# Result stores of one batch's 64 rows each, in place of stores over two batches' 128 rows

## The chip, the cores and the metric

The kernel runs on one core of a Trainium2 chip. A core has a matrix engine (PE, whose weight loads are shown as PEld), three engines for elementwise work (DVE, ACT, POOL), a queue engine (SP) that here does nothing but start DMAs, and 16 DMA engines that carry them out. The metric is the device time of one execution in microseconds (us); the median over runs is given, lower is better.

## The reference, cut to what matters

Two blocks follow each other: a linear attention with a decaying state (4 batches, 8 heads, 768 steps, 48 features a head) and a feed-forward block on its 3072 output rows of 384 features.

```python
B, H, S, D = 4, 8, 768, 48                       # then 3072 rows, d_model 384, d_ff 1536
for t in range(S):
    cur = einsum('bhd,bhe->bhde', u[None] * k[:, :, t], v[:, :, t])
    y[:, :, t] = einsum('bhd,bhde->bhe', r[:, :, t], state + cur)
    state = w[None, :, :, None] * state + einsum('bhd,bhe->bhde', k[:, :, t], v[:, :, t])
x = y.transpose(0, 2, 1, 3).reshape(B * S, H * D)  # row b*768 + t
xn = x / sqrt(mean(x * x) + 1e-6) * rms_g
g = xn @ w_gate
out = (g * sigmoid(g) * (xn @ w_val)) @ w_out
```

The weights of the second block arrive as float64, the rest as float32.

## The kernel before

**Tiling.** Time is cut into 12 chunks `s` of 64 steps (`L`); one chunk holds 64 rows of each of the 4 batches, 256 rows of the result. `mixing(s)` does the attention of a chunk, and the feed-forward block then runs on it. Chunks 0 and 1 go through it one by one; chunks 2 to 11 go in pairs (s, s+1), five pairs, where a scheme with seven products in place of eight replaces the plain block products. For a pair, `group(s, m)` makes the first layer for six slices m (products `f1` to `f7` on PE in the PSUM banks a, b and c, copies and activations on ACT, sums on DVE), and `second_layer(s)` the second (products `P1` to `P7`).

**Order of the work.** All operations of all engines are listed in a plan with costs and due times, and the plan is then given out as one fixed order for each engine. Each engine works strictly in that order, so an operation whose input is late also holds up everything behind it on its engine. Every DMA is started by SP in its order; an instruction of SP that starts one shows as `DMA_DIRECT2D`. Nearly all instructions are recorded on line L92, the helper that gives them out, so groups are told apart by tile names.

**The results.** `second_layer` leaves the 256 x 2 result rows of a pair in the tile `rows_out`, seen as `results[:, k, j]`: 128 partitions; k is one of four quarters (chunk s or s+1, first or second half of the 384 features); j is a pair of batches. The partitions hold batch 2j in rows 0 to 63 and batch 2j+1 in rows 64 to 127. A quarter becomes ready by a sum on DVE or a copy on ACT, and `result(k, chunk, f, js)` then stores it: keys r0, r2, r3 and r1, in this order; r1 last, behind the last product. For the last pair, r1 is made and stored for the two values of j apart (`js` is (0,) and then (1,)). Chunks 0 and 1 have a store of their own (`store`), with DMAs of 64 rows of 384 features; it is not touched.

**The looks.** The kernel also verifies that the float64 weights are in a range that its fast path takes. It loads them in 36 pieces of 384 KB into the tile `sq` (the function `check`; below, such a piece is called a look), and two ACT operations read each piece (`Abs`, and `Relu` with an accumulated sum, followed by a short read of the accumulator). A look's DMA overwrites the one before, so SP waits for the ACT operations of the look before it. Five looks belong to each `mixing` from chunk 2 on, until the 36 are through. They stand in the order of SP between the stores, and in the order of ACT between the activations of the groups.

**The end.** A flag `bad` is summed up from the looks; all engines load it as a number and branch on it (L1149, L1602). SP loads it between the stores of r3 and those of r1 of the last pair.

Of the kernel before, what the change touches and what calls it, by code (L numbers as in the profile page):

```python
# [55 lines left out]
def free_dims(t, *dims):  # L56

    return bass.AP(tensor=t.tensor, offset=t.offset, ap=[list(t.ap[0])] + [list(d) for d in dims])
# [3 lines left out]
B, H, S, D = 4, 8, 768, 48  # L62
HP = H // 2
L = 64
NS = S // L
DM, DFF = H * D, 1536
# [28 lines left out]
class Plan:  # L95
# [11 lines left out]
    def add(self, engine, cost, reads, writes, give, land=0.0, port=False, name="", rows=False):  # L107


        deps = {self.last[r] for r in reads if r in self.last} | {self.last[w] for w in writes if w in self.last}  # L110
        for w in writes:
            deps |= self.readers.get(w, set())
        n = len(self.ops)
        if engine in ("DVE", "ACT"):
            cost += 0.03
        self.ops.append((engine, cost, deps, give, land, port, name, rows))
        for w in writes:
            self.last[w], self.readers[w] = n, set()
        for r in reads:
            if r not in writes:  # L120
                self.readers.setdefault(r, set()).add(n)
        return n
# [114 lines left out]
def fast(ctx, tc, chan, tok, vpad, wka, wkb, wot, cols, u_row, out, bad):  # L237
# [8 lines left out]
    pe, dve, act, pool, sp = (InOrder(tc, e) for e in (nc.tensor, nc.vector, nc.scalar, nc.gpsimd, nc.sync))  # L246
# [46 lines left out]
    for z in range(2):  # L293
        rows = slice(64 * z, 64 * z + 64)
        pool.affine_select(
            out=mask[rows], in_=mask[rows], compare_op=ALU.is_ge, fill=0.0, base=-1, pattern=[[1, L]],
# [324 lines left out]
    HALF = DM // 2  # L621
# [51 lines left out]
    add = lambda *args, **kwargs: p.add(*args, **kwargs)  # L673
# [391 lines left out]
    def second_layer(s):  # L1065

        keys = {"x": "a0", "w": "a1", "y": "b0", "z": "c0", "v": "c1"}
        bank = {t: bank_of[key[0]][:, int(key[1])] for t, key in keys.items()}
        flat = {t: bank[t][:, 0:DM].rearrange("p (j f) -> p j f", j=2) for t in bank}
        sum_1 = lambda: late["gv"].rearrange("p a b t -> p (a b) t")[:, 0 : NN // 2]  # L1070
        sum_2 = lambda: free_dims(late["t"], (NT, NN // 2), (1, NT))
        m1 = lambda: free_dims(late["m1"], (HALF, 2), (1, HALF))
        h = [H_ALL[:, :, k] for k in range(4)]
        h_keys = [[f"h{m}.{k}" for m in range(NN // 2)] for k in range(4)]
        results = rows_out.rearrange("p s j f -> p (s j f)").rearrange("p (c j f) -> p c j f", c=4, j=2)
        w2 = lambda n: lambda i, o: late["w2"][:, n, i, o]
        part = lambda q, f: lambda i, o: wo[i + q][:, o, f * HALF : (f + 1) * HALF]

        def mm(t, reads, left, right, start, name, js=(0, 1), ms=range(NN // 2)):
            def give():  # L1080
                for j in js:
                    for m in ms:
                        pe.matmul(
                            flat[t][:, j], left()[:, m, j * P : (j + 1) * P], right(*divmod(m, NQ)),
                            start=start and m == 0 and j == js[0], stop=m == NN // 2 - 1, skip_group_check=True,
                        )

            line.append(add("PE", 0.325 * len(js) * len(ms), reads, [keys[t]], give, name=f"{name} {s}"))

        def result(k, chunk, f, js=(0, 1)):  # L1090
            def give():
                for j in js:
                    to = bass.AP(
                        tensor=out.tensor, offset=out.offset + (2 * j * S + chunk * L) * DM + f * HALF,
                        ap=[[S * DM, 2], [DM, L], [1, HALF]],
                    )
                    sp.dma_start(out=to, in_=results[:, k, j])

            add("SP", 0.6 * len(js), [f"r{k}"], [], give, name="store")

        def plus(writes, reads, to, x, y, name):
            add("DVE", 0.55, reads, writes, lambda: dve.tensor_add(to, x, y() if callable(y) else y), name=name)

        out_keys = lambda *ns: [f"{n}.{i}" for n in ns for i in range(2)]
        gs, ts = [f"g{k}" for k in range(4)], ["t1", "t2"]
        add("DVE", 1.66, h_keys[1] + h_keys[3], gs, lambda: dve.tensor_add(sum_1(), h[1], h[3]), port=True, name="sum_1")
        add("DVE", 1.66, h_keys[0] + gs, ts, lambda: dve.tensor_sub(sum_2(), sum_1(), h[0]), port=True, name="sum_2")
        add("DVE", 1.66, h_keys[0], h_keys[1], lambda: dve.tensor_sub(h[1], h[0], h[1]), port=True, name="sum_3")
        for ms in (range(NN // 2 - 1), range(NN // 2 - 1, NN // 2)):
            mm("x", [h_keys[0][m] for m in ms], lambda: h[0], part(0, 0), ms[0] == 0, "P1", ms=ms)  # L1110
        add("ACT", 0.47, ["a0"], ["m1"], lambda: act.copy(m1(), flat["x"]), name="m1")
        mm("z", gs + out_keys("o1"), sum_1, w2(0), True, "P5")
        mm("x", h_keys[2], lambda: h[2], part(2, 0), False, "P2")
        add("ACT", 0.47, ["a0"], ["r0"], lambda: act.copy(results[:, 0], flat["x"]), name="c11")
        result(0, s, 0)
        add("DVE", 1.66, ts, h_keys[2], lambda: dve.tensor_sub(h[2], h[2], sum_2()), port=True, name="sum_4")
        mm("y", ts + out_keys("o2"), sum_2, w2(1), True, "P6")
        plus(["r1"], ["b0", "m1"], results[:, 1], flat["y"], m1, "u2")
        plus(["r1"], ["c0"], results[:, 1], flat["z"], results[:, 1], "u4")
        mm("w", h_keys[3] + out_keys("o4"), lambda: h[3], w2(2), True, "P4")  # L1120
        mm("y", h_keys[1] + out_keys("o3"), lambda: h[1], part(0, 1), False, "P7")
        plus(["r3"], ["b0", "m1"], results[:, 3], flat["y"], m1, "u3")
        plus(["r2"], ["a1", "r3"], results[:, 2], flat["w"], results[:, 3], "c21")
        result(2, s + 1, 0)
        plus(["r3"], ["c0"], results[:, 3], flat["z"], results[:, 3], "c22")
        result(3, s + 1, 1)
        for js in ((0, 1),) if s + 2 < NS else ((0,), (1,)):
            mm("v", h_keys[2], lambda: h[2], part(2, 1), js[0] == 0, "P3", js)
            to, x = (t[:, js[0] : js[-1] + 1] for t in (results[:, 1], flat["v"]))
            plus(["r1"], ["c1"], to, x, to, "c12")  # L1130
            result(1, s, 1, js)
# [536 lines left out]
```

## Time and profile before

| what | value |
|---|---|
| median of 3 runs | 657.22 us (656.98 to 657.53) |
| the profiled execution, own time | 654.39 us |
| its span, first to last instruction | 652.6 us |
| PE busy | 613.1 us, 94% of the span |
| DVE, ACT, POOL busy | 437.8, 354.3, 42.8 us |
| DMA | 62.92 MB moved, mean 96 GB/s |
| stores from `rows_out` | 48 DMAs of 96 KB |

Of the profile, the page gives sums over the span and a bar for each engine in 40 slices of 16.3 us, each digit a tenth of the slice. The timeline lists instructions in order of time: start, duration, engine, operation, output and input tile, count, and in brackets the idle time before it with what ended it. The chain of work that ended last goes back from the end, step by step to what released each step. A table of windows gives, for stretches of time, the busy time of each engine, the granted TensorE clock (1.00 is full speed), the mean busy share of the 16 DMA engines and the rate.

### The profile page before, as it was taken

What the parts mean: (1) busy time and instruction counts of PE and PEld (TensorE: products, weight loads), DVE (VectorE), ACT (ScalarE), POOL (GpSimd) and SP (SyncE); (2) the same over time, 40 slices, a digit from 0 to 9 for tenths busy, and PEclk for the clock granted to TensorE, in tenths of its full rate; (3) what the DMA queues carried; (4) which work ended last, traced back from release to release, by engine and by line L of the source; (5) the groups of instructions that cost most, each with busy time, mean ns of one, the idle gap of its engine ahead of it and who ended that gap; (6) DMA issues with size and microseconds to landing.
All of it is one profiled execution on the core that took longest, in us unless ns stands there. A gap on an engine that the chain in (4) does not pass through costs nothing.

```text
span 652.6 us, 15362 instructions
## 1 busy us (share of the span) xinstructions
PE 613.1 (94%) x6544; PEld 540.8 (83%) x6544; DVE 437.8 (67%) x621; ACT 354.3 (54%) x895; POOL 42.8 (7%) x41
## 2 busy tenths in 40 slices
PE   8979999999999996899999699999999989999991
PEld 8867787777888995788998488899888889888991
DVE  7888877877867972477884268795557865555620
ACT  6988578674596355448757327948222872222100
POOL 2255324000000000000000000000000000000000
PEclk9989999999999999799999799999999999999997
DMA  8687744117115122042612232341004101000001
GB/s 292 219 320 213 235 174 157 67 49 229 45 29 176 66 68 84 25 147 80 191 35 84 62 87 96 97 143 52 29 1 147 39 2 30 26 2 1 1 13 42
DMA packets 22190, 62.92 MB, mean 96 GB/s; under 512 B 2560, under 2 KB 9568, under 8 KB 20704
## 3 DMA queue, kind: packets, MB, share of 16 engines
q1 hardware_dynamic: 22112, 61.85, 29.8%
q8 instruction: 53, 0.87, 0.6%
q14 instruction: 25, 0.20, 0.1%
HBM read 55.94 MB, written 4.72 MB: 93 GB/s over the span
## 4 chain that ended last, share of the span: by engine, by line
PE 82%; DMA 7%; ACT 5%; DVE 2%; SPq 1%; issue 1%; POOL 0%; ACTq 0%; POOLq 0%
PE bank_b L92 27%; PE bank_a L92 25%; PE bank_c L92 21%; PE at L92 10%; DMA sq<-in_wka_dram 2%; DMA sq<-in_wot_dram 2%; DMA VS<-in_vpad_dram 1%; DMA raw<-in_wka_dram 1%; SPq L92 1%; ACT sq L92 1%; ACT L92 1%; ACT MO L92 1%; ACT VS L92 1%; ACT ME L92 1%; DVE h L92 1%
## 5 line engine op out<-in xcount | busy, mean ns | idle before, releaser
L92 DVE TENSOR_TENSOR gv<-bank_b,m 128x512 f32<-128x512 f32 x90 | 62.1, 690 | 71.7 <-PE bank_b L92 66.0
L92 PE MATMUL bank_a<-xa,wa 64*128 64x256 f32 x396 | 52.2, 398 | 14.4 <-DVE h L92 14.4
L92 ACT ACTIVATE sq<-sq 128x384 f32<-128x384 f32 x72 | 40.2, 559 | 39.6 <-DMA sq<-in_wka_dram 16.6
L92 PEld LDWEIGHTS bank_a<-xa,wa 64*128 64x128 f32 x396 | 38.7, 195 | 21.8 <-DVE h L92 15.2
L92 PE MATMUL bank_b<-xa,wa 64*128 64x256 f32 x444 | 55.2, 381 | 1.2 <-DVE gv L92 1.2
L92 ACT ACTIVATE gv<-gv 128x512 f32<-128x512 f32 (+1 forms) x60 | 31.1, 523 | 38.4 <-DVE gv L92 38.1
L92 PE MATMUL bank_a<-wo,h 128*128 128x192 f32 (+1 forms) x264 | 49.4, 343 | 2.0 <-DVE h L92 2.0
L92 ACT ACTIVATE gv<-bank_a 128x256 f32<-128x256 f32 x30 | 11.5, 383 | 71.5 <-PE bank_a L92 71.3
L92 DVE TENSOR_TENSOR gv<-bank_c,gv 128x512 f32<-128x512 f32 x60 | 41.4, 690 | 12.3 <-PE bank_c L92 11.0
L92 PEld LDWEIGHTS bank_b<-xa,wa 64*128 64x128 f32 x444 | 41.9, 187 | 8.4 <-DVE gv L92 2.4
L92 PE MATMUL bank_a<-xb,wb 64*128 64x256 f32 x396 | 48.6, 378 | 0.0
L92 PEld LDWEIGHTS bank_a<-wo,h 128*128 128x128 f32 x264 | 43.5, 190 | 6.2 <-DVE h L92 2.1
L92 ACT ACTIVATE ME<-dmask,du 64x64 f32<-64x64 f32 x176 | 45.8, 331 | 4.2 <-DVE du L92 3.5
L92 ACT ACTIVATE MO<-dmask,du 64x64 f32<-64x64 f32 x176 | 46.5, 339 | 0.4
L92 PE MATMUL bank_b<-t,s 64*128 64x256 f32 x360 | 45.7, 388 | 0.0
L92 PE MATMUL bank_b<-t,wb 64*128 64x256 f32 x360 | 44.7, 381 | 0.4 <-DVE gv L92 0.4
L92 PE MATMUL bank_c<-t,s 64*128 64x256 f32 x360 | 44.1, 377 | 0.0
L92 PE MATMUL bank_c<-xb,s 64*128 64x256 f32 x360 | 43.8, 376 | 0.0
L92 PEld LDWEIGHTS bank_a<-xb,wb 64*128 64x128 f32 x396 | 38.0, 187 | 5.0 <-issue 0.5
L92 ACT COPY m<-bank_a 128x512 f32<-128x512 f32 (+1 forms) x35 | 19.9, 567 | 40.9 <-PE bank_a L92 38.7
L92 PEld LDWEIGHTS bank_b<-t,s 64*128 64x128 f32 x360 | 36.3, 196 | 4.8
L92 PEld LDWEIGHTS bank_c<-t,s 64*128 64x128 f32 x360 | 34.6, 187 | 4.9 <-issue 0.5
(152 smaller groups left out, 1257.2 us busy)
## 6 DMA issues: line engine op xcount, KB each, us to landing
chan<-in_chan_dram SPq DMA_DIRECT2D x11, 1024.0 KB
TOK<-in_tok_dram SPq DMA_DIRECT2D x11, 768.0 KB
VS<-in_vpad_dram SPq DMA_DIRECT2D x24, 256.0 KB
raw<-in_wot_dram SPq DMA_DIRECT2D x8, 576.0 KB
sq<-in_wka_dram SPq DMA_DIRECT2D x12, 384.0 KB
sq<-in_wkb_dram SPq DMA_DIRECT2D x12, 384.0 KB
sq<-in_wot_dram SPq DMA_DIRECT2D x12, 384.0 KB
out_dram<-rows_out SPq DMA_DIRECT2D x48, 96.0 KB
```

What stands on the lines that cost most here:

```text
L92: return lambda *args, **kwargs: self.tc.keep_in_program_order(give(*args, **kwargs))
```

## The change

Each store of a quarter was two DMAs, one for each pair of batches j; each took all 128 partitions, so its target in memory was two blocks of 64 rows, 768 rows apart. Now it is two DMAs, one for each half of the partitions (bl is 0 or 1); each takes the 64 rows of one batch for both values of j. Size and number stay: 96 KB, pieces of 768 bytes. Where `js` has one entry (r1 of the last pair, twice), one DMA of 128 rows becomes two of 64 rows and 48 KB. The plan's cost of a store stays 1.2 for the stores with both values of j and goes from 0.6 to 1.2 for the last two.

```diff
         def result(k, chunk, f, js=(0, 1)):
             def give():
-                for j in js:
+                for bl in range(2):
                     to = bass.AP(
-                        tensor=out.tensor, offset=out.offset + (2 * j * S + chunk * L) * DM + f * HALF,
-                        ap=[[S * DM, 2], [DM, L], [1, HALF]],
+                        tensor=out.tensor, offset=out.offset + ((2 * js[0] + bl) * S + chunk * L) * DM + f * HALF,
+                        ap=[[DM, L], [2 * S * DM, len(js)], [1, HALF]],
                     )
-                    sp.dma_start(out=to, in_=results[:, k, j])
-
-            add("SP", 0.6 * len(js), [f"r{k}"], [], give, name="store")
+                    sp.dma_start(out=to, in_=results[bl * L : (bl + 1) * L, k, js[0] : js[-1] + 1])
+
+            add("SP", 1.2, [f"r{k}"], [], give, name="store")
```

On PE, DVE, ACT and POOL the order of the instructions up to the branch is the same as before. On SP, the stores change their shape and two are added. The first place is the store of the pair (4, 5), on SP: `out_dram<-rows_out` are the stores, `sq<-` the looks; x4 are the two of r3 and the two of r1.

```order
-L92 DMA out_dram<-rows_out 2x64x192 x2
-L92 DMA sq<-in_wot_dram 128x384
-L92 DMA out_dram<-rows_out 2x64x192 x2
-L92 DMA sq<-in_wka_dram 128x384
-L92 DMA out_dram<-rows_out 2x64x192 x4
+L92 DMA out_dram<-rows_out 64x2x192 x2
+L92 DMA sq<-in_wot_dram 128x384
+L92 DMA out_dram<-rows_out 64x2x192 x2
+L92 DMA sq<-in_wka_dram 128x384
+L92 DMA out_dram<-rows_out 64x2x192 x4
 L92 DMA sq<-in_wka_dram 128x384 x2
```

Nothing moves against the looks here; the slowest dimension of the stores' target goes from 2 to 64. The second place is the end of the program on SP, before:

```order
L92 DMA out_dram<-rows_out 2x64x192 x14
L1149 TENSOR_LOAD bad
L1149 ISA x2
L92 DMA out_dram<-rows_out 2x64x192 x2
L1602 COMPARE_AND_BRANCH
```

And the same place with the change:

```order
L92 DMA out_dram<-rows_out 64x2x192 x14
L1149 TENSOR_LOAD bad
L1149 ISA x2
L92 DMA out_dram<-rows_out 64x192 x4
L1602 COMPARE_AND_BRANCH
```

Behind the load of the flag stand four stores of 64 rows in place of two of 128.

## The prediction

> **What bounds the kernel now.** I read the bars of the page first. PE is the bottleneck, so only slices in which it idles matter.
>
> ```profile
> PE   8979999999999996899999699999999989999991
> PEclk9989999999999999799999799999999999999997
> ```
>
> PE is full except at the start, in the 16th and 17th slices (from 245 us), in the 23rd (from 359 us), a little in the 33rd, and in the last. In the slice after each of the two long gaps the granted clock is down as well. The timeline of PE gives the two gaps and what ended them, and a small one ahead of the first:
>
> ```profile
> 250.35 1.57 PE L92 MATMUL bank_b<-xa,wa 64*128 64x256 f32 x12 [0.60 <-DVE gv L92]
> 263.72 2.93 PE L92 MATMUL bank_a<-xa,wa 64*128 64x256 f32 x12 [7.92 <-DVE h L92]
> 369.10 2.93 PE L92 MATMUL bank_a<-xa,wa 64*128 64x256 f32 x12 [6.52 <-DVE h L92]
> ```
>
> Call them stall A (255.80 to 263.72) and stall B (362.58 to 369.10). The chain of work that ended last shows what DVE was late for: a look, and ahead of it an SP that could not start its next DMA.
>
> ```profile
> 250.87 1.96 SPq L92
> 252.93 7.30 DMA sq<-in_wka_dram
> 268.69 1.29 PE bank_c L92 x12
> ...
> 355.44 2.65 SPq L92
> 358.19 7.42 DMA sq<-in_wka_dram
> 374.28 1.29 PE bank_c L92 x12
> ```
>
> In both, 3.49 us lie between the landing (252.93 + 7.30 = 260.23; 358.19 + 7.42 = 365.61) and PE's restart: two ACT passes over the look, a table load, the activation that PE's bank waits for, a DVE product. ACT's order is fixed, so the activation can't overtake the look. SP's timeline shows the stores in front:
>
> ```profile
> 246.85 1.88 SPq L92 DMA_DIRECT2D out_dram<-rows_out  x1
> 248.83 1.99 SPq L92 DMA_DIRECT2D out_dram<-rows_out  x1
> 252.93 2.27 SPq L92 DMA_DIRECT2D sq<-in_wka_dram  x1
> 354.84 0.55 SPq L92 DMA_DIRECT2D out_dram<-rows_out  x1
> 355.44 2.65 SPq L92 DMA_DIRECT2D out_dram<-rows_out  x1
> 153.36 2.45 SPq L92 DMA_DIRECT2D out_dram<-rows_out  x4
> 406.26 0.33 SPq L92 DMA_DIRECT2D sq<-in_wkb_dram  x1
> ```
>
> A store's start takes 0.55 us when SP is free and up to 2.65 us behind others. The last two rows are yardsticks: the untouched 64-row stores of chunk 1 (four in 2.45 us, 0.61 each, none held up), and a look with no store about. Why stores hold things up is in the windows (columns: length; busy time of PE, PEld, DVE, ACT, POOL; granted clock; busy share of the 16 DMA engines; GB/s):
>
> ```profile
> 248.50:252.50 4.00, 3.40 (x32) 2.73 (x30) 1.23 (x2) 3.95 (x15) 0.00 (x0) 1.00 0.14 46
> 255.50:257.50 2.00, 0.30 (x4) 0.00 (x0) 0.00 (x0) 0.00 (x0) 0.00 (x0) 1.00 0.75 219
> 257.50:260.00 2.50, 0.00 (x0) 0.00 (x0) 0.00 (x0) 0.00 (x0) 0.00 (x0) 1.00 0.13 45
> 153.50:157.50 4.00, 4.00 (x66) 3.42 (x64) 3.12 (x4) 0.30 (x1) 0.00 (x0) 1.00 0.91 322
> 157.50:159.00 1.50, 1.50 (x38) 1.39 (x36) 0.81 (x2) 1.16 (x4) 0.00 (x0) 1.00 0.05 12
> ```
>
> While only stores run, the share is 0.14, about 2 of 16 engines, at 46 GB/s: one 96 KB store drains in 2.1 us. The look bursts through most engines in 255.5 to 257.5 (0.75), and then 2.5 us pass at two engines' rate, where its last shares wait behind stores. The chunk-1 stores, whose target has 64 rows as its slowest dimension, ran in the 0.91 stretch (with loads) and were gone by 159: had they had only two engines, four issued by 155.8 would have taken 8.5 us from their start. So the target's leading 2 is what confines a store, and the new leading 64 should free it.
>
> The Trainium skill (DMA: Bandwidth & Descriptors, Why a DMA increments its semaphore by 16 and not by 1) gives the rule: the number of engines is the largest up to 16 that divides the slowest dimension of both sides. The 0.14 agrees with its 2; for the new stores it says 16, and the sum below would be the same by it.
>
> **The change, part by part.** The stores at 234, 341, 447 and 544 us have no PE wait behind them but for A and B; three places count.
>
> *Stall A.* The last quarter is ready when DVE's sum ends, at 247.04 + 0.55 = 247.59:
>
> ```profile
> 247.04 0.55 DVE L92 TENSOR_TENSOR rows_out<-bank_c,rows_out 128x384 f32<-128x384 f32 x1
> 247.88 1.14 ACT L92 ACTIVATE sq<-sq 128x384 f32<-128x384 f32 x2
> 410.72 1.16 ACT L92 ACTIVATE sq<-sq 128x384 f32<-128x384 f32 x2 [0.72 <-DMA sq<-in_wkb_dram]
> ```
>
> A new store's start is unknown; between 0.55 (unhindered old ones) and 0.61 (64-row ones, the nearest row) I take 0.61. Two end at 248.81. The look needs also the look before it read, which ACT ends at 249.02 at the latest; the start moves from 252.93 to about 248.85, at worst 249.1. Its flight without stores is 406.26 to about 410.68, 4.42 us. It lands at 253.27, and PE restarts 3.49 later, at 256.76 in place of 263.72: **-7.0**. The stall left is 256.76 - 255.80 = 1.0, or some 1.6, as the 0.60 gap at 250.35 can close when the looks ahead come sooner; that doesn't move the restart.
>
> *The clock after A and B.* After each stall PE crawls:
>
> ```profile
> 263.72:266.00 2.28, 2.28 (x10) 1.86 (x12) 2.17 (x4) 1.45 (x4) 0.00 (x0) 0.50 0.12 47
> 255.90:263.60 7.70, 0.00 (x0) 0.00 (x0) 0.36 (x2) 3.23 (x8) 0.00 (x0) 0.84 0.35 98
> 362.60:369.00 6.40, 0.00 (x0) 0.00 (x0) 0.38 (x2) 2.83 (x5) 0.00 (x0) 0.84 0.21 65
> PE bank_a L92 <- DVE h L92: 2.0, 1, 2.0
> 525.40:529.00 3.60, 3.57 (x22) 3.58 (x23) 3.50 (x4) 3.52 (x14) 0.00 (x0) 1.00 0.00 0
> ```
>
> A mean of 0.84 over 7.7 us between 1.00 and 0.50 puts the drop 5.2 us into stall A; over 6.4 us, 4.4 us into B. The 2.0 us stall before 525.4 kept the full clock. The first two cells of 12 matmuls took 268.69 - 263.72 = 4.97 after A and 374.28 - 369.10 = 5.18 after B; at 1.29 each with 0.1 for the restart they take 2.7. If the stalls left stay near 2 us this is saved: **-2.3** and **-2.5**.
>
> *Stall B.* The first store of the last quarter started at 354.84; two at 0.61 end at 356.06, the look starts at 356.1 in place of 358.19, lands at 360.5, PE restarts at 364.0 in place of 369.10: **-5.1**. The stall left is 1.4 to 2.1.
>
> *The end.* Here PE is done and SP is the path:
>
> ```profile
> 636.96 2.39 SPq L92 DMA_DIRECT2D out_dram<-rows_out  x1
> L1149 SPq TENSOR_LOAD <-bad x1: 2458/2458/2458, 639.4 to 639.4; - x1
> 638.95 0.36 DVE L92 TENSOR_TENSOR rows_out<-bank_c,rows_out 128x192 f32<-128x192 f32 x1 [2.26 <-PE bank_c L92]
> 642.29 1.73 SPq L92 DMA_DIRECT2D out_dram<-rows_out  x2
> L1602 SPq EVENT_SEMAPHORE  x8: 17/17/17, 646.9 to 651.2; - x8
> ```
>
> The store at 636.96 blocks SP for 2.39, the flag's load takes 2.46 and 0.43 follow to the next store; the last of SP's closing waits passes at 651.2, and the span ends 1.4 later at 652.6. With the change: 636.96 + 0.61 + 2.46 + 0.43 = 640.46 (DVE is done at 639.31), then four stores of 0.61, two more than before, which cost 1.2 here; the last starts at 642.29. Its landing is unknown. The four at 153.36 started their last at 155.2, and traffic had faded at 157.5, so 2.3; I take 2.5, between 1.7 and the 4.42 of a look four times its size. 644.8 + 1.4 = 646.2: **-6.4** (-4.5 to -7.2).
>
> Starts of the other stores hide behind SP's long waits (the longest kind below); if that cover went, each would cost 0.06 more than the old 0.55.
>
> ```profile
> SPq L92 <- PE at L92: 156.6, 23, 29.9
> ```
>
> Late next are the rest of A and B, and ACT, which then fetches the following look just in time.
>
> Sum: -7.0 - 2.3 - 5.1 - 2.5 - 6.4 = -23.3 us. The execution of the trace took 654.39, 1.8 over its span, so it would take 631.1. The median shown is 2.8 above that execution; taken off the median, **633.9**.
>
> **Rivals.** (1) *Looks stay slow behind spread stores*: now every engine has store pieces ahead of the look. The dearest look with 64-row stores ahead is this, with 1.3 MB of loads ahead too:
>
> ```profile
> 150.67 6.44 DMA sq<-in_wot_dram
> ```
>
> At 6.44 in place of 4.42, A and B gain 4.0 less (637.9); the stalls left, 3.0 to 4.1, approach the 4.4 at which the clock fell, and losing that too gives 642.7. Against it: new stores bring 0.4 MB there.
> (2) *Only the end gains*, because something else holds ACT in A and B: 657.2 - 6.4 = 650.8. The chain names the looks in both, so little speaks for it.
> (3) *The change doesn't spread the stores*, since their second dimension is still 2: 657.2. The chunk-1 stores have no such dimension, so they don't exclude it.
> (4) *Slower: 64 partitions are a slower source.* Should a store drain at half of 46 GB/s, 23, the six stores before look A (0.59 MB, 12.8 us) would take 12.8 more, the four before look B 8.5, the six at the end 12.8: 691. It decides as soon as a store takes over 2.1 us to drain. Against it stand 322 GB/s with the chunk-1 stores in the mix. The Trainium skill speaks for it (SBUF — State Buffer, Door 1: The DMA port swizzle): 64 partitions reach only 8 of the 16 ports, so two DMAs of half the partitions lose bandwidth to one over all. No run here shows ports.
>
> **How the numbers follow.** My forecast has 0.65 (its own range 630 to 638), rival 1 0.19 (638 to 645), rival 2 0.06, rival 3 0.05, rival 4 0.04; 0.01 for gains below 630. The low end: a flight 0.8 shorter in both stalls and -7.2 at the end give 631.5, with some slack 630; the high end takes in rival 1 at 645. Within 0.2% (1.3 us) is about what a measurement of this kernel can't tell from no change. Faster by more: 0.65 + 0.19 + 0.06 + 0.01 = 0.91; same 0.05; slower 0.04.
>
> **What would show it.** In the changed kernel's profile: no store's start over about 0.7 us on SP; a high DMA share right after a store instead of 0.14; looks in A and B that fly 4 to 5 us; PE gaps of 1 to 2 us with the clock at 1.00 behind them; and 7 us instead of 13 between the last DVE sum and the end. It is wrong if stores still drain at 46 GB/s, if a look's flight stays above 6 us, or if the clock falls in stalls of 2 us.

## The result, and the profile after

The changed kernel takes **634.18 us** (median of 4 runs, 631.83 to 638.04) against 657.38 us (656.98 to 657.95, 4 runs) before: a ratio of 0.9652, 95% interval 0.9601 to 0.9703, or -23.2 us. The prediction was 633.9 us in a range of 630 to 645. The profiled execution took 633.14 us, with a span of 631.4 us.

The page first: the bars of PE and of the granted clock.

```profile
PE   8979999999999999999999899999999989999994
PEclk9998999999999999999999899999999999999998
```

The two deep notches of before (slices 16, 17 and 23) are gone; a small one is left in slice 23, with a dip of the clock in the same slice. The list of PE's waits (total, times, longest) puts a number on it, first of before, then of after:

```profile
PE bank_a L92 <- DVE h L92: 16.4, 3, 7.9
```

```profile
PE bank_a L92 <- DVE h L92: 5.2, 3, 2.2
```

PE's timeline shows what is left of the two stalls:

```profile
256.52 1.57 PE L92 MATMUL bank_a<-xa,wa 64*128 64x256 f32 x12 [0.95 <-DVE h L92]
257.92 1.46 PE L92 MATMUL bank_b<-t,s 64*128 64x256 f32 x12
259.21 0.60 PE L92 MATMUL bank_c<-t,s 64*128 64x256 f32 x4
...
354.61 2.44 PE L92 MATMUL bank_a<-xa,wa 64*128 64x256 f32 x12 [2.24 <-DVE h L92]
356.84 2.32 PE L92 MATMUL bank_b<-t,s 64*128 64x256 f32 x12
```

Stall A went from 7.92 to 0.95 us, stall B from 6.52 to 2.24 us. Behind A the first two cells take 259.21 - 256.52 = 2.69 us, at full clock; behind B they take 4.39 us (to 359.00), because the clock still fell, about 0.5 us after PE had started again (last section). SP's timeline and the chain of work that ended last give the cause:

```profile
L92 SPq DMA_DIRECT2D out_dram<-rows_out x40: 489/602/847, 243.0 to 625.9; - x40
248.91 0.61 SPq L92 DMA_DIRECT2D out_dram<-rows_out  x1
249.62 0.55 SPq L92 DMA_DIRECT2D sq<-in_wka_dram  x1
345.54 1.25 SPq L92 DMA_DIRECT2D out_dram<-rows_out  x2
346.88 1.27 SPq L92 DMA_DIRECT2D sq<-in_wka_dram  x1
```

```profile
249.62 3.38 DMA sq<-in_wka_dram
...
346.88 4.22 DMA sq<-in_wka_dram
```

From 242 us on, the 40 stores start in 602 ns (median), 847 ns at most, where before they took up to 2.65 us; the looks fly 3.38 and 4.22 us instead of 7.30 and 7.42. In the windows (the last two numbers are the share of the 16 DMA engines and GB/s), two stores that start at 431.74 and 432.44 with little else about:

```profile
433.00:433.50 0.50, 0.50 (x5) 0.50 (x5) 0.50 (x1) 0.50 (x3) 0.00 (x0) 1.00 0.77 161
434.00:434.50 0.50, 0.50 (x5) 0.50 (x4) 0.00 (x0) 0.50 (x3) 0.00 (x0) 1.00 0.51 105
```

The share is 0.51 to 0.77 in place of 0.14. The end shows in SP's rows:

```profile
L1149 SPq TENSOR_LOAD <-bad x1: 757/757/757, 622.6 to 622.6; - x1
623.83 2.79 SPq L92 DMA_DIRECT2D out_dram<-rows_out  x4
L1602 SPq EVENT_SEMAPHORE  x8: 17/17/17, 629.5 to 630.0; - x8
```

The last four stores start from 623.83, and the closing waits pass by 630.0. Two rows of DVE make a yardstick that is free of a disturbance in all comparisons, that the program's start is not equally long in every execution. The first sum into `rows_out` (chunk 0) and the last `bank_b` sum (last pair) bound a **middle**; from the last sum into `rows_out` to the end of the span is the **tail**.

```profile
L92 DVE TENSOR_TENSOR rows_out<-bank_c,rows_out x18: 348/554/958, 77.0 to 623.8; 128x384 f32<-128x384 f32 x14, 128x768 f32<-128x768 f32 x2, 128x192 f32<-128x192 f32 x2
L92 DVE TENSOR_TENSOR rows_out<-bank_b,m x10: 550/558/559, 230.3 to 618.8; 128x384 f32<-128x384 f32 x10
```

Here the middle is 618.8 - 77.0 = 541.8 and the tail 631.4 - 623.8 = 7.6; 5.0 to 5.1 us lie between them in every run. The same rows of every profiled execution:

| run | start | middle | tail | median, us | ratio to before |
|---|---|---|---|---|---|
| before | 76.4 | 557.5 | 13.7 | 657.38 | 1 |
| changed kernel | 77.0 | 541.8 | 7.6 | 634.18 | 0.9652 [0.9601, 0.9703] |
| changed kernel again (x1_after) | 81.2 | 540.9 | 7.3 | 635.4 | 0.9679 [0.9638, 0.9719] |
| new stores in the first two pairs only (e1_first_two) | 78.4 | 541.0 | 13.6 | 640.2 | 0.976 [0.972, 0.9799] |
| new stores in the last pair only (e2_last_pair) | 80.8 | 558.4 | 7.2 | 648.39 | 0.9874 [0.9837, 0.9911] |
| after without looks (e4_after_nolook) | 77.4 | 537.9 | 7.5 | 629.19 | 0.959 [0.955, 0.963] |
| before without looks (e5_before_nolook) | 78.5 | 537.7 | 13.9 | 637.12 | 0.9718 [0.9677, 0.9759] |
| 128 rows, leading 4 (r5_lead4) | 77.4 | 547.6 | 8.1 | 641.27 | 0.9764 [0.9739, 0.9788] |
| 128 rows, leading 128 (r3_128rows) | 77.5 | 540.6 | 5.8 | 630.16 | 0.9593 [0.9557, 0.963] |
| last stores shared with ACT (e7_act_end) | 79.3 | 543.2 | 6.2 | 632.74 | 0.9621 [0.9595, 0.9648] |

The start differs by up to 4.8 us between these executions, of the same kernel too (77.0 and 81.2). It makes the second profiled execution of the changed kernel the longer one (634.5 against 631.4 us), though its middle and tail are shorter; how much of the spread of the other runs it makes (631.83 to 638.04) is not shown. Before to after, the middle gives -15.7, the tail -6.1, and the start costs 0.6: -21.2 us, the difference of the spans (652.6 to 631.4).

### The profile page after: what moved, and what is told of

Its sections match the earlier page's. It is cut to its first block, busy times and chain, and to the rows that moved or that the text cites. A ratio compares the mean times of both kernels' runs of the same rounds, so it can differ in the third digit from the quotient of the medians.

```text
span 631.4 us, 15364 instructions
## 1 busy us (share of the span) xinstructions
PE 610.4 (97%) x6544; PEld 539.4 (85%) x6544; DVE 437.6 (69%) x621; ACT 355.1 (56%) x895; POOL 42.9 (7%) x41
## 4 chain that ended last, share of the span: by engine, by line
PE 89%; ACT 4%; DMA 3%; DVE 2%; issue 1%; SPq 0%; POOL 0%; ACTq 0%; POOLq 0%
PE bank_b L92 28%; PE bank_a L92 26%; PE bank_c L92 24%; PE at L92 10%; DMA sq<-in_wka_dram 1%; DMA sq<-in_wot_dram 1%; ACT L92 1%; DMA VS<-in_vpad_dram 1%; ACT sq L92 1%; DVE rows_out L92 1%; ACT VS L92 1%; DVE h L92 1%; SPq L92 0%; ACT MO L92 0%; ACT yT L92 0%
## 5 line engine op out<-in xcount | busy, mean ns | idle before, releaser
L92 PE MATMUL bank_a<-xa,wa 64*128 64x256 f32 x396 | 50.4, 387 | 3.2 <-DVE h L92 3.2
L92 PE MATMUL bank_b<-wo,h 128*128 128x192 f32 (+1 forms) x168 | 38.4, 385 | 1.8 <-DVE h L92 1.8
```

The costliest lines, as they stand in the source:

```text
L92: return lambda *args, **kwargs: self.tc.keep_in_program_order(give(*args, **kwargs))
```

## The experiments

The theory: a store whose target leads with 2 runs on about 2 of the 16 DMA engines; while such stores drain, SP's next start and the next look are late, ACT's fixed order passes that on to PE (A and B), and the same slow stores stretch the end. The rivals: the shape of 64 rows matters and not the spread; something else than the looks stands behind A and B; the gain lies in the end alone.

### One part of the change alone

The new form only in the first two pairs, and only in the last. The rest is as before.

```diff
+                if s in (2, 4):      # e2_last_pair: if s == 10:
                     for bl in range(2):
                         ...          # the new form
+                else:
+                    for j in js:
+                        ...          # the old form
```

> Only the stores of the pairs (2,3) and (4,5) have the new form, those of the other three pairs the old one. Theory (a store whose target has a leading dimension of 2 runs on two DMA engines, holds up SP and the look behind it, and so PE in the stalls A and B): A and B gain as in the whole change, 7.8 + 2.3 for A with its clock, 5.2 + 0 to 2.5 for B: 15 to 18 us, a time of 640 to 642; the end stays as before, about 13 us from the last DVE sum to the end. Rival (only the end gains): no change, 657.

> Only the stores of the last pair (10,11) have the new form. Theory: stalls A and B stay at about 7.9 and 6.5 us, the end shortens by 6 to 7 us: 650.5 to 651.5. Rival (only the end gains, all of it): 634. With the run of the first two pairs it should add up to the whole change within 1 us, so that the stores of the pairs (6,7) and (8,9) are worth nothing.

Measured: 640.2 us and 648.39 us, against 655.98 us of the kernel before on the same chip: -15.8 and -7.6. The first is in its range; the second is 2.1 us below its range, though its tail gains the 6.5 us that were expected (its runs go from 647.37 to 653.2). The two add up to -23.4, the whole change. In the profiles the parts separate fully: with the first two pairs the middle falls to 541.0 and the tail stays at 13.6; with the last pair the middle stays at 558.4 and the tail falls to 7.2. PE's timeline of the last-pair kernel has both stalls still in it:

```profile
267.79 2.50 PE L92 MATMUL bank_a<-xa,wa 64*128 64x256 f32 x10 [8.18 <-DVE h L92]
373.98 2.93 PE L92 MATMUL bank_a<-xa,wa 64*128 64x256 f32 x12 [6.54 <-DVE h L92]
```

"Only the end gains" is refuted. The rows of SP's flag load, first of the first-two-pairs kernel, then of the last-pair kernel, show something that the prediction had as fixed:

```profile
L1157 SPq TENSOR_LOAD <-bad x1: 2448/2448/2448, 625.0 to 625.0; - x1
```

```profile
L1157 SPq TENSOR_LOAD <-bad x1: 777/777/777, 643.1 to 643.1; - x1
```

With old stores ahead of it the load of one number takes 2.45 us, with new ones 0.78.

### The looks taken out

From the 11th look on, the DMA is left out, in the changed kernel and in the one before. ACT still makes its two passes over the tile, without the short read of the accumulator (0.19 us); these weight pieces are not verified.

```diff
+    pool.memset(seen, 0.0)
 ...
-            "SP", 0.95, [], keys, lambda: sp.dma_start(out=raw, in_=...), land=LAND,
+            "SP", 0.95, [], keys, (lambda: sp.dma_start(out=raw, in_=...)) if n < 10 else (lambda: None), land=LAND,
 ...
-            lambda: act.activation(hi, hi, AF.Relu, scale=-(2.0**15), bias=1.0, accum_out=seen[:, n : n + 1]),
+            (the same) if n < 10 else (lambda: act.activation(hi, hi, AF.Abs)),
```

> The changed kernel, with the DMA of the 11th to 36th look left out; ACT still makes two passes over the tile (both Abs), so ACT's load stays and only the wait for the look goes; those weight pieces are not verified. Theory: the rests of A (0.95) and B (2.24) and the clock lost after B vanish: 3 to 6 us less than the changed kernel, 628 to 631; and if the changed kernel's spread between runs (631.8 to 638.0) comes from the clock falling or not in these short stalls, the runs here lie within 1.5 us. Rival (the spread comes from the stores or the end): the spread stays near 6 us.

> The kernel before (old stores) with the same 26 looks' DMAs left out; those weight pieces are not verified. Theory: without looks behind them the slow stores harm nothing but the end: A and B vanish with their clock, 7.9 + 6.5 + 4.8 = 19 us: 637 to 639, and the distance to the changed kernel without looks is the end alone, 6 to 7 us. Rival (slow stores hold up PE in other ways too): over 10 us between the two.

Measured: 629.19 us with the new stores and 637.12 us with the old ones, both in the ranges expected. The first kernel's runs lie 2.4 us apart (628.72 to 631.12), neither the 1.5 of the theory on the spread nor the 6 of its rival, so that question stays open. The bars of PE, first of the old stores without looks, then of the new ones:

```profile
PE   8979999999999999999999999999999899999991
```

```profile
PE   8979999999999999999999999999999989999994
```

With the looks gone, A and B are gone with the old stores too, and the middles are alike, 537.7 and 537.9. So in the middle the form of the stores acts on PE through the looks and, to within these 0.2 us, through nothing else. Of what stays between the two kernels, 7.9 us by medians and 7.3 by spans, 6.4 lie behind the last sum (tails of 13.9 and 7.5), and 1.1 of the spans in the start. The changed kernel's middles of 541.8 and 540.9 also show what the looks still cost there: 3 to 4 us.

### Spread against shape

Two kernels keep stores of 128 partitions and, against the kernel before, change only the target (and the plan's cost of the last two stores, to the 1.2 of the change). In one its slowest dimension is 4 (four blocks of 32 rows), in the other 128 (one unbroken block). In both the rows land in other places of the output. The edit is shown against the changed kernel.

```diff
-                for bl in range(2):
+                for j in js:
 ...
-                        ap=[[DM, L], [2 * S * DM, len(js)], [1, HALF]],
+                        ap=[[S * DM, 4], [DM, L // 2], [1, HALF]],   # r3_128rows: [[DM, 2 * L], [1, HALF]]
 ...
-                    sp.dma_start(out=to, in_=results[bl * L : (bl + 1) * L, k, js[0] : js[-1] + 1])
+                    sp.dma_start(out=to, in_=results[:, k, j])
```

> As the run before it, but the 128 rows go to four blocks of 32 rows, one in each batch, so the slowest dimension is 4; the rows inside a chunk land in each other's place. Theory: four engines, a busy share of 0.25 to 0.28 and about 92 GB/s while only stores run; a store drains in 1.05 us, SP is hardly held up, looks land 1 to 2 us later than in the changed kernel, the end is 0 to 3 us longer: 634 to 642, between the two kernels and nearer the new. Rival (64 rows): 655 to 658.

> The old division (one DMA for each pair of batches, all 128 partitions of two batches, 96 KB), but the 128 rows go to one unbroken block of the result, so the target's slowest dimension is 128 and not 2; odd chunks of even batches and even chunks of odd batches land in each other's place. Theory (only the target's leading dimension sets the number of engines): as fast as the changed kernel or, with two stores fewer at the end, 1 us better: 631 to 636. Rival (one batch's 64 rows are what counts): 655 to 658. The rate while only stores run tells besides what 64 partitions cost: the changed kernel has about 150 GB/s at a busy share of 0.7; if 128 partitions are faster, this shows over 200.

Measured: 641.27 us, in its range, and 630.16 us, 0.8 below its range. With a leading 4, PE's timeline, the chain, a window in which only a store runs, and SP's rows:

```profile
258.73 1.99 PE L92 MATMUL bank_a<-xa,wa 64*128 64x256 f32 x12 [2.99 <-DVE h L92]
359.66 2.93 PE L92 MATMUL bank_a<-xa,wa 64*128 64x256 f32 x12 [3.38 <-DVE h L92]
```

```profile
249.65 5.57 DMA sq<-in_wka_dram
350.89 5.26 DMA sq<-in_wka_dram
```

```profile
441.00:441.50 0.50, 0.50 (x5) 0.50 (x4) 0.12 (x1) 0.49 (x3) 0.00 (x0) 1.00 0.27 92
```

```profile
L1149 SPq TENSOR_LOAD <-bad x1: 2107/2107/2107, 628.7 to 628.7; - x1
```

A share of 0.27 is 4.3 of 16 engines, at 92 GB/s, twice the 0.14 and 46 GB/s of a leading 2. Stalls, flights, the flag's load and the middle (557.5, 547.6, 541.8 for 2, 4 and 64) all lie between before and after. The Trainium skill (DMA: Bandwidth & Descriptors, Why a DMA increments its semaphore by 16 and not by 1) gives the largest number up to 16 that divides the slowest dimension of both sides; the shares 0.14 and 0.27 agree with its 2 and 4 of 16.

With the unbroken block, in the same views:

```profile
355.64 1.57 PE L92 MATMUL bank_a<-xa,wa 64*128 64x256 f32 x12 [1.74 <-DVE h L92]
```

```profile
432.00:432.50 0.50, 0.50 (x5) 0.50 (x5) 0.50 (x2) 0.49 (x3) 0.00 (x0) 1.00 0.66 211
432.50:433.00 0.50, 0.50 (x5) 0.50 (x5) 0.50 (x1) 0.50 (x4) 0.00 (x0) 1.00 0.48 155
```

```profile
L92 SPq DMA_DIRECT2D out_dram<-rows_out x48: 332/424/1387, 147.3 to 623.6; - x48
L1150 SPq TENSOR_LOAD <-bad x1: 488/488/488, 621.5 to 621.5; - x1
```

So 64 rows are not what helps: 128 rows, spread, gain as much and a little more. Two such stores drain in about 1.0 us (155 to 211 GB/s) where two of 64 rows take about 1.5 us (105 to 161), start in 0.42 us instead of 0.60, and the tail is 5.8 instead of 7.6, with two stores fewer to start there. By the medians alone, whose intervals overlap, the two kernels can't be told apart. The reference's layout does not allow this form, since the two batches of a `j` lie 768 rows apart.

### What is left: the last stores and the late looks

Two edits were tried on top of the change. In the first, ACT, idle by then, starts the second of each two last stores. In the second, the plan is told that a look flies 3.5 us, where it had 2.1 (`LAND`) and the traces show 3.4 to 4.2 at A and B.

```diff
-                    sp.dma_start(out=to, in_=results[...])
+                    queue = act if bl and len(js) == 1 else sp
+                    queue.dma_start(out=to, in_=results[...])
 ...
-            "SP", 0.95, [], keys, lambda: sp.dma_start(...), land=LAND,
+            "SP", 0.95, [], keys, lambda: sp.dma_start(...), land=3.5,
```

e7_act_end has the first edit, x2_land35 the second, e8_land_act and x3_land_act (the same kernel) both; x1_after is the changed kernel again.

> The changed kernel, with the second of each two 48 KB stores at the very end started by ACT and not by SP. Theory (at the end SP's starts, four of about 0.55 to 0.75 us, are the path): 1 us less than the changed kernel, 633. Rival (the landing of the last store and the closing waits set the end): no change, 634; or slower by up to 1 if ACT's start waits behind its own load of the flag.

> As the run before it, and the plan takes a look's flight as 3.5 us and not 2.1 (with 0.95 for its start), near the 4.2 to 4.4 measured, so that it puts ACT's passes over a look later than other work. The order on all engines may change. Theory (the rests of A and B are ACT waiting for a look whose flight the plan underrates): the PE gaps of 0.95 and 2.24 shrink below 0.5 in sum, 2 to 5 us less, 629 to 632. Rival (another order puts the wait elsewhere): 633 to 640.

> The changed kernel once more, beside the two runs after it on one chip: 632 to 636. Its rest of stall B is 2.2 to 2.4 us long; once the clock fell behind such a stall (changed kernel) and once it held (the run with the first two pairs), so either can come.

> The changed kernel with the plan's flight of a look at 3.5 and not 2.1, SP alone starting the last stores. Theory (the rests of A and B are worth 3 us and the clock behind B another 0 to 2.5): 1 to 4 us less than the changed kernel, 630 to 633. Rival (the new order gives it back in other PE waits): the same within 1 us.

> Both edits, the plan's flight and the last stores shared out to ACT: 0 to 1 us less than the run before it, 629 to 633.

| run | start | middle | tail | median, us | ratio to before |
|---|---|---|---|---|---|
| e8_land_act | 76.1 | 544.4 | 6.0 | 632.06 | 0.9613 [0.9588, 0.9638] |
| x2_land35 | 76.5 | 544.6 | 7.8 | 636.15 | 0.9686 [0.9651, 0.9722] |
| x3_land_act | 76.3 | 543.1 | 6.3 | 633.57 | 0.965 [0.9617, 0.9682] |
| x4_late_land_act | 81.3 | 541.6 | 6.1 | 634.87 | 0.9656 [0.9619, 0.9693] |

Against what was expected, x1_after is in its range, e8_land_act and x3_land_act lie just above theirs, x2_land35 gave its rival's result (no gain), and the median of e7_act_end can't decide between 633 and 634. The shared start shows in the tail every time: 6.0 to 6.3 us in the four kernels with it, 7.2 to 7.8 in the five that have new stores at the end, all started by SP. The longer flight takes the wait at B away and leaves one of 0.81 us near A. From the first pair's `bank_b` sum to the end of the middle these three kernels take 383.3 to 385.0 us, the changed kernel in its two profiles 388.5 and 386.5. But the plan, which searches its order with these numbers, moves other work: that first sum stands 159.4 to 159.8 us behind the first chunk's, against 153.3 and 154.4. So the middle is 543.1 to 544.6, against 540.9 to 543.2 with the old flight (e7_act_end has the highest of these). The last try, with the first edit too, kept the plan's search as it is and used 3.5 us only behind it, for the looks from the eleventh on:

```diff
+    for i, op in enumerate(p.ops):
+        if op[0] == "SP" and op[6].startswith("look ") and int(op[6][5:]) >= 10:
+            p.ops[i] = op[:4] + (3.5,) + op[5:]
+    p.then = []
```

> The changed kernel, with the last stores' second halves started by ACT (as in the run where that was done alone), and with the plan's flight of a look set to 3.5 us instead of 2.1 us only for the looks from number 10 on, after the search for the order, so that the first phase keeps the order that it has in the changed kernel. Theory (the two stalls that are left, 0.95 to 1.57 and 2.2 to 2.4 us, are a matter of the plan thinking a look lands after 2.1 us where it takes 3.4 to 4.2 us; the loss of the earlier runs with 3.5 us came from the first phase's other order): the first pair's last sum stands 153 us after the first chunk's, as in the changed kernel, from there to the last u3 sum 384 to 386 us instead of 388.5, the tail 6.2 us: 629 to 632 us. Rival (the second phase's new order gives back what the stalls gave, or the spread of the program's start covers it): 633 to 636 us.

It measured 634.87 us: the rival's result. The theory was right on the tail (6.1) and on the stretch from the first pair's sum to the end of the middle (384.7), but the first pair's sum stood 156.9 us behind the first chunk's and not 153, so the middle is 541.6, just as in the changed kernel. The order had drawn work forward: in the 155 us from the first sum on, ACT is busy for 114.0 us there and for 101.8 in the changed kernel. That the earlier work on ACT is what delays that sum is not shown. None of these versions can be told from the changed kernel by its median; only the saving of 1.3 us in the tail is shown, in the traces.

## Why the prediction was right

The forecast case came true. That its sum of 23.3 us meets the 23.2 us measured to 0.1 is partly luck: in the traces its terms make 22.2, with -7.0 for A a little small and -2.5 for the clock after B much too large, and the medians add what the profiled executions differ by (below). By its own steps, with times of before's frame found by taking off how much earlier or later the same group of PE runs ahead of each stall and of the small gap in front of it (0.63 us later at A, 246.23 against 245.60; 9.31 us earlier at B, 343.04 against 352.35):

1. **What bounds the kernel** (a look behind slow stores): right. Without looks the middle does not depend on the stores (537.7 and 537.9).
2. **The target's leading 2 confines a store**: right, by the leading 4 (92 GB/s, stalls of 2.99 and 3.38 us) and by the 128 rows that are spread (540.6).
3. **Stall A, -7.0**: measured -7.8. The look starts at 249.62 - 0.63 = 248.99 (predicted 248.85), flies 3.38 us where 4.42 was taken, and PE restarts 3.52 us behind the landing (3.49). The small gap ahead closed, as was said.
4. **Stall B, -5.1**: measured -5.2; the look flies 4.22 us, and PE restarts 3.51 us behind it.
5. **The clock after A, -2.3**: measured 4.97 - 2.69 = -2.28.
6. **The clock after B, -2.5**: mis-sized. It was 5.18 - 4.39 = -0.8 in the profiled execution. The step's condition, that a stall near 2 us keeps the clock, did not hold for 2.24 us, so one of the prediction's own signs of being wrong came true; it held in other runs. The step took the length of the stall for what decides, and the traces show that where the stall lies decides too (last section). In the changed kernel's second profile the clock held, and its middle is 0.9 us shorter.
7. **The end, -6.4**: measured -6.1, but two terms were off and cancelled. The flag's load was taken over at 2.46 us and was 0.76; so the last store started 2.1 us behind the start of DVE's last sum (625.9 - 623.8) and not 3.3. On the other side 2.5 us were taken from the last start to the last closing wait, and it was 630.0 - 625.9 = 4.1.
8. **The other stores at no cost**: right; no wait of PE came up at them.
9. **"No store's start over about 0.7 us"**: not quite. The median was 0.60, but single starts reached 0.85 from 242 us on, and 1.39 at the first pair's second store (235.8 us).

Of the rivals, (1) would have shown looks of over 6 us at A and B: they fly 3.38 and 4.22, and only the flight with leading 4 came near (5.57). (2) fell with the first-two-pairs kernel, which gains 15.8 us with the end as before; (3) with the windows. (4) has a true core, a store of 64 partitions is slower than one of 128 when both are spread, by about 1.5 to 1.0 us for two; but it is far over 46 GB/s. The Trainium skill (SBUF — State Buffer, Door 1: The DMA port swizzle) says that 64 partitions reach half of the ports; the runs agree in direction, show two thirds of the rate rather than a half, and no ports.

By spans the terms of the trace (-7.8, -2.3, -5.2, -0.8, -6.1) make -22.2. The longer start takes 0.6 back, 0.4 are small differences elsewhere, and the spans differ by 21.2. The medians differ by 2.0 more, since before's profiled execution was 3.0 us below its median and after's 1.0.

## What to carry to other kernels

Read the DMA share in a stretch where only one kind of transfer runs: 0.14 at 46 GB/s is two engines at work, and the outermost dimension of the target says why. Small slow stores cost nothing by themselves; they cost where something on the critical path stands behind them on the same queue or in the same DMA engines, here a look, an ACT order that can't go round it, and a flag's load. When a fixed order is searched with a guessed flight time, correcting the guess need not pay: the wait moves.

## What the runs showed of the hardware that was not expected

**A register load takes longer behind slow stores.** The load of one number took 2.46 us (before), 2.45 (old stores at the end) and 2.11 (leading 4), but 0.76 and 0.78 (64-row stores) and 0.49 (128 rows, spread). What in the load waits is not shown.

**When the clock falls is not set by the length of the stall alone.** The windows behind stall B in four kernels; the column ahead of the DMA share is the clock. First after (a stall of 2.24 us), then the changed kernel again (2.09), the first-two-pairs kernel (2.40), and leading 4 (3.38):

```profile
354.61:359.00 4.39, 4.39 (x25) 3.62 (x27) 2.17 (x4) 2.69 (x6) 0.00 (x0) 0.61 0.07 28
```

```profile
359.64:363.60 3.96, 3.96 (x36) 3.58 (x38) 2.86 (x5) 2.69 (x6) 0.00 (x0) 1.00 0.07 26
```

```profile
356.94:361.00 4.06, 4.06 (x38) 3.66 (x40) 2.85 (x5) 2.70 (x6) 0.00 (x0) 1.00 0.07 26
```

```profile
359.66:364.90 5.24, 5.24 (x24) 4.24 (x26) 2.17 (x4) 2.69 (x6) 0.00 (x0) 0.50 0.06 24
```

2.24 us cost the clock, 2.40 us did not, and the same kernel kept it once and lost it once. In finer windows the traces show why.

In each of the fourteen profiles the clock is 1.00 or 0.50, and its changes lie whole multiples of 3.41 us apart, from the first to the last (in the changed kernel falls at 47.95, 355.15 and 628.22, 90 and 80 beats apart): it changes on a fixed beat. In the changed kernel it is 1.00 through the whole of stall B (352.37 to 354.61), falls at 355.15 and is back at 358.56, one beat later; before, it stayed down for two beats behind A (261.20 to 268.02) and behind B (367.01 to 373.84).

These are single beats, with PE's busy time in the third column: first before, the last two beats ahead of the fall in stall A; then the changed kernel at its fall; then the changed kernel again, and the two beats over which the stall of the first-two-pairs kernel lies.

```profile
254.37:257.78 3.41, 1.43 (x14) 0.94 (x10) 0.00 (x0) 0.00 (x0) 0.00 (x0) 1.00 0.53 152
257.79:261.20 3.41, 0.00 (x0) 0.00 (x0) 0.00 (x0) 0.86 (x2) 0.00 (x0) 1.00 0.08 30
```

```profile
351.74:355.15 3.41, 1.17 (x10) 0.70 (x10) 1.01 (x3) 2.31 (x4) 0.00 (x0) 1.00 0.40 115
355.15:358.56 3.41, 3.41 (x19) 2.73 (x17) 1.63 (x4) 2.45 (x5) 0.00 (x0) 0.50 0.00 0
```

```profile
355.85:359.26 3.41, 1.71 (x16) 1.17 (x14) 0.10 (x1) 2.86 (x5) 0.00 (x0) 1.00 0.21 44
```

```profile
352.31:355.72 3.41, 2.22 (x22) 1.64 (x18) 0.00 (x0) 2.17 (x4) 0.00 (x0) 1.00 0.14 50
355.72:359.13 3.41, 2.19 (x20) 2.00 (x22) 2.58 (x5) 2.29 (x6) 0.00 (x0) 1.00 0.40 114
```

PE's idle time is 3.41 less its busy time. The 2.24 us of the changed kernel lie in one beat; of the 2.09 us in its second profile 1.70 lie in one beat, and the 2.40 us of the first-two-pairs kernel are split into 1.19 and 1.22. From 60 us on, in all fourteen profiles, a beat with up to 1.90 us of idle never cost the clock and one with 2.00 us or more always did; between these both happened (1.99 ahead of stall A's fall cost nothing).

Where the beat lies against the stall differs from execution to execution, so a stall of 2.0 to 2.4 us loses the clock or keeps it by chance. A fall cost 1.7 us behind B (4.39 against 2.69) and 2.3 and 2.5 us before. One more is found near 510 us in e7_act_end, e8_land_act, x2_land35, x4_late_land_act and both kernels without looks, and in neither profile of the changed kernel; it is part of what sets their middles apart.

The Trainium skill (TensorE: Matmul & The Clock Gate, What's actually happening) has a window of about 3.4 us that runs freely, so that it matters where in it a stall falls. The traces agree with the 3.41 us of their beat; its one full idle window does not fit the falls after 2.24 us of idle.
